# A written-out order for the first 1400 operations, early loads that wait for older ones, and masks and coefficients stored behind unit 0's values

## The chip, the cores and the metric

The kernel runs on one core of a Trainium2 chip. The core has a matrix engine (PE), a vector engine (DVE), an activation engine (ACT), a general engine (POOL) and a queue engine (SP) that issues transfers; each runs its own instructions strictly in the order in which they were written, and waits on semaphores for the others. 16 DMA engines move the data. The metric is device time in microseconds (us) per execution, lower is better.

## The reference

Attention over 8 batches, 8 heads, 576 positions and 64 features, with a local mask (32 keys back for half of the heads, 32 keys in steps of 4 for the others), and behind it a two-layer network whose activation is a rational function with learned coefficients:

```python
scores = np.where(masks, q @ k.T / 8, -1e9)
x = softmax(scores) @ v                 # (4608 tokens, 512)
h = x @ w_in                            # 512 -> 2048
P = a[0] + a[1]*h + a[2]*h**2 + a[3]*h**3
Q = 1 + abs(b[0])*abs(h) + abs(b[1])*h**2
out = (P / (Q + 1e-6)) @ w_out          # 2048 -> 512
```

`w_in` and `w_out` arrive in 64 bits and are turned into 32-bit numbers on the core.

## The kernel before, in words

**Units.** The attention is cut into 48 units, six for each of 8 batches (unit n = 6b + u). A unit loads its queries and keys (`qk`, 448 KB) and its values (`v`, 384 KB); then PE adds the mask and makes scores, DVE takes the maximum (`mx`), ACT the exponential, DVE the sum (`sm`) and its reciprocal, POOL or ACT divides (`p`), PE transposes (`t`, copied to `pT`), PE multiplies with `v`, and the result is split into a high and a low half, `xh` and `xl`. Units 0 to 5 (batch 0) write their halves straight from PSUM; the later ones go through DRAM (`results<-y`, then `z<-results`).

**Weights.** 16 blocks of `w_in` (`wi`) and 16 of `w_out` (`wo`), 512 KB each. Every block is loaded (`wi_raw`), scaled on ACT (`wi_f`), joined with its low bits (a multiply and shift on DVE), copied to a high half (ACT, DVE or POOL) and subtracted to a low half (DVE or POOL).

**Tiles.** 9 groups of 512 tokens times 16 blocks give 144 tiles. For each, PE makes `h` in 12 matmuls of 128x512; ACT and DVE work out the rational function (on DVE five passes at the least: `t<-t,h`, `h<-t,na_t,h`, `h<-h,na_t,r`, `a<-a,r`, `a<-a,h`; the product `a<-r,a` and the low half `gl` go to DVE or POOL); and PE adds the tile into four sums in 12 more matmuls (`out`). The first 8 tiles use batch 0, the next 16 batch 1, then the rest of batch 0, and so on. `h` and the transposes `t` share two PSUM banks in turn, so transpose 11, the last of the units of batch 1, waits until DVE is done with tile 1, and tile 2's `h` comes right behind it.

**What sets the order.** All work is a list of operations with an allowed set of engines, a cost and a due time (`Plan.op`). `Plan.run` steps through it before anything runs: it looks for the operation that can start first by its own costs, among those within 200 ns takes the one that is due first, and records its instructions. What is recorded on an engine stays in that order. Where PE would wait in the plan, before 150 us of it, `keep_busy` records matmuls on constants that nobody reads (128x512 bf16, of `ident_b`). All loads and stores are issued from SP through `load` and wait there for nothing but buffers and data.

Of the kernel before, what the change touches and what calls it, by code (L numbers as in the profile page):

```python
# [25 lines left out]
BOTH = {"ACT": 480, "DVE": 520}  # L26
# [5 lines left out]
DUE = [(-38.49, 8.95), (-134.53, 10.99), (409.06, 77.81), (48.99, 2.72), (456.65, -31.55), (557.24, -11.85), (83.16, -17.62), (714.91, 29.14)]  # L32

LATE = {"ab": -275.92, "ql": -296.25, "pl": 24.3, "qq": -47.45, "t1": 94.47, "t2": -169.93, "ln": 295.15, "ex": -497.79, "g0": -1.51, "g1": -59.76, "g2": -270.73, "gh": -314.62, "gl": 497.37, "out": 3.78}
SLACK = {"sc": 1.16, "qk0": -46.44, "v0": -50.35, "load": -3.46, "wi": 11.08, "wo": -0.87, "w": -17.68, "gl": -7.82, "out": -4.87}
# [4 lines left out]

DEPTH, LOADS, STAGE, AHEAD, ON_PE, BY_PE = 2, 2, 6, 6, 2, 2
LEFT = S - 512
RQ, RKEY, NV = 4 * 3 * 32, 4 * 128, 3 * 2 * 2 * 64
# [18 lines left out]

class Op:
# [4 lines left out]
    def __init__(self, engs, rank, fn, deps, dma, lock):  # L68
        self.engs, self.rank, self.fn, self.dma, self.lock = engs, rank, fn, dma, lock
        self.deps = [d for d in deps if d is not None]  # L70
        self.takes, self.follows = [], []
        self.spare = None
# [9 lines left out]
class Plan:  # L82
# [7 lines left out]
    DMA_START, DMA_NS, DMA_RATE = 1000.0, 1700.0, 380.0  # L90
# [5 lines left out]
    def op(self, engs, rank, fn, *deps, dma=0, lock=False):  # L96
        o = Op(engs, rank, fn, deps, dma, lock)
        self.ops.append(o)
        return o
# [32 lines left out]
    def run(self):  # L132
        free = {}
        pipe, ports = self.DMA_START, 0.0
# [6 lines left out]
        ready = [o for o in self.ops if not left[id(o)]]  # L141
        done = 0
        while ready:
            options = []
            for o in ready:
                before = list(o.deps)
                for tag, _ in o.takes:
                    bufs, groups = self.tags[tag]
                    if len(groups) >= bufs:
                        users = groups[len(groups) - bufs]  # L150
                        if any(u.end is None for u in users):
                            break
                        before += users
                else:
                    for eng, ns in o.engs.items():
                        shared = ports if Plan.shares(o, eng) else 0.0
                        t = max([free.get(eng, 0.0), shared] + [d.after(eng) for d in before])
                        options.append((t, o, eng, ns))
# [943 lines left out]
```

## Time and profile before

| | |
|---|---|
| runs | 913.08, 913.37, 917.36 us; median 913.37 us |
| profiled execution | span 911.9 us from first to last instruction; the median run is 1.5 us more than this span, which is taken as what lies around it |
| PE busy | 887.7 us (97%) |
| DVE, ACT, POOL busy | 727.6, 684.8, 472.8 us |
| moved | 103.46 MB, mean 113 GB/s |

A busy PE is no measure of work done here, since the matmuls on constants count too, and a matmul at half clock counts double. What matters is at which time a given tile starts, and which engine had no idle time before it.

### The profile page before, as it was taken

How to read it: one execution, taken by the hardware profiler on the slowest of the kernel's cores; microseconds unless marked ns; L12 is line 12 of the kernel's file. 1: busy time of each engine (PE TensorE's matmuls, PEld its weight loads, DVE VectorE, ACT ScalarE, POOL GpSimd, SP SyncE). 2: the span in 40 equal slices, each digit the busy share in tenths (PEclk: the TensorE clock that was granted, in tenths of full speed). 3: DMA queues.
4: the chain of work that ended last, by engine and by line, in shares of the span. 5: the costliest groups of instructions: out<-in, count | busy, mean ns of one | idle time of the engine just before them, and what ended most of it. 6: DMA issues, size and time to landing. Idle time of an engine off the chain costs nothing.

```text
span 911.9 us, 21320 instructions
## 1 busy us (share of the span) xinstructions
PE 887.7 (97%) x8208; PEld 714.9 (78%) x8208; DVE 727.6 (80%) x1291; ACT 684.8 (75%) x1128; POOL 472.8 (52%) x424
## 2 busy tenths in 40 slices
PE   6889999999999999999999999999999999999998
PEld 4656778877887888888888878888888888888876
DVE  4889999988998986888688886887688677566656
ACT  3888899867767777677767767777877788778774
POOL 2354666635555654555555555456455555544442
PEclk8899999999999999999999999999999999999999
DMA  9785614144643531453155441233143220001001
GB/s 339 272 281 181 241 55 147 60 127 143 192 141 113 152 93 46 131 165 112 49 173 156 135 141 65 96 104 98 47 145 108 63 70 1 0 1 47 1 1 46
DMA packets 85478, 103.46 MB, mean 113 GB/s; under 512 B 37377, under 2 KB 62849, under 8 KB 85377
## 3 DMA queue, kind: packets, MB, share of 16 engines
q1 hardware_dynamic: 85376, 102.11, 35.1%
q8 instruction: 64, 1.05, 0.5%
q14 instruction: 38, 0.30, 0.1%
HBM read 75.21 MB, written 26.87 MB: 112 GB/s over the span
## 4 chain that ended last, share of the span: by engine, by line
PE 82%; DVE 8%; DMA 4%; ACT 2%; issue 2%; POOL 1%; SPq 1%; DVEq 0%; ACTq 0%; POOLq 0%
PE out L245 39%; PE h L245 38%; PE pair L245 4%; DVE a L254 2%; DMA results<-y 1%; DVE h L254 1%; DMA z<-results 1%; ACT r L248 1%; DMA qk<-in_qk_dram 1%; DVE t L251 1%; SPq L242 1%; POOL a L257 1%; PE pair_A L245 0%; DVE a L251 0%; PE pair_B L245 0%
## 5 line engine op out<-in xcount | busy, mean ns | idle before, releaser
L245 PE MATMUL h<-xh,wi 128*128 128x512 f32 x1136 | 376.7, 393 | 5.5 <-DVE a L254 5.1
L245 PE MATMUL out<-gh,wo 128*128 128x512 f32 x1136 | 352.8, 392 | 0.0
L257 POOL TENSOR_TENSOR a<-r,a 128x512 f32<-128x512 f32 x123 | 159.2, 1294 | 259.4 <-ACT r L248 241.2
L245 PEld LDWEIGHTS h<-xh,wi 128*128 128x128 f32 x1136 | 213.3, 188 | 55.2 <-DVE a L254 9.3
L245 PEld LDWEIGHTS out<-gh,wo 128*128 128x128 f32 x1136 | 211.6, 188 | 44.9
L245 PE MATMUL out<-gl,wo 128*128 128x512 f32 x568 | 221.4, 390 | 0.6 <-POOL gl L257 0.6
L245 PE MATMUL h<-xl,wi 128*128 128x512 f32 x568 | 221.3, 390 | 0.0
L257 POOL TENSOR_TENSOR gl<-a,gh 128x512 fp32r<-128x512 f32 x137 | 182.0, 1329 | 40.9 <-ACT gh L248 31.0
L254 DVE SCALAR_TENSOR_TENSOR a<-a,r 128x512 f32<-128x512 f32 x141 | 101.4, 719 | 121.3 <-ACT r L248 119.3
L248 ACT ACTIVATE r<-a,ln_bias 128x512 f32<-128x512 f32 x141 | 101.8, 722 | 67.9 <-POOL a L257 64.5
L248 ACT ACTIVATE r<-a,ab_t 128x512 f32<-128x512 f32 x141 | 114.6, 813 | 14.6 <-DVE h L254 9.0
L245 PEld LDWEIGHTS out<-gl,wo 128*128 128x128 f32 x568 | 106.6, 188 | 23.7 <-POOL gl L257 1.2
L245 PEld LDWEIGHTS h<-xl,wi 128*128 128x128 f32 x568 | 106.7, 188 | 21.3
L248 ACT ACTIVATE a<-h 128x512 f32<-128x512 f32 x140 | 83.3, 595 | 52.4 <-PE h L245 44.2
L254 DVE SCALAR_TENSOR_TENSOR h<-t,na_t,h 128x512 f32<-128x512 f32 x142 | 107.3, 755 | 4.6
L248 ACT ACTIVATE t<-h,na_t 128x512 f32<-128x512 f32 x142 | 109.2, 769 | 1.6 <-DVE h L254 1.2
L254 DVE SCALAR_TENSOR_TENSOR h<-h,na_t,r 128x512 f32<-128x512 f32 x142 | 106.5, 750 | 4.6 <-ACT r L248 3.3
L248 ACT ACTIVATE r<-r,exp_bias 128x512 f32<-128x512 f32 x144 | 104.3, 724 | 4.7
L248 ACT ACTIVATE gh<-a 128x512 fp32r<-128x512 f32 x133 | 83.6, 628 | 27.0 <-PE out L245 24.5
L251 DVE TENSOR_TENSOR t<-t,h 128x512 f32<-128x512 f32 x142 | 95.9, 675 | 5.9 <-ACT t L248 4.9
L254 DVE SCALAR_TENSOR_TENSOR a<-a,h 128x512 f32<-128x512 f32 x140 | 96.2, 687 | 4.8
L257 POOL TENSOR_TENSOR xl<-z,xh 128x256 fp32r<-128x256 f32 (+5 forms) x52 | 39.1, 764 | 33.1 <-ACT xh L248 32.7
(123 smaller groups left out, 716.2 us busy)
## 6 DMA issues: line engine op xcount, KB each, us to landing
qk<-in_qk_dram SPq DMA_DIRECT2D x48, 448.0 KB, 5.3
v<-in_vp_dram SPq DMA_DIRECT2D x48, 384.0 KB, 3.9
out_dram<-os SPq DMA_DIRECT2D x36, 256.0 KB, 2.1
wi_raw<-in_w_in_dram SPq DMA_DIRECT2D x16, 512.0 KB, 6.2
wo_raw<-in_w_out_dram SPq DMA_DIRECT2D x16, 512.0 KB, 5.9
results<-y SPq DMA_DIRECT2D x42, 192.0 KB, 3.5
z<-results SPq DMA_DIRECT2D x168, 48.0 KB, 2.0
turned<-u SPq DMA_DIRECT2D x36, 192.0 KB, 2.2
```

The source lines that it names most:

```text
L242: pin(nc.sync.dma_start(dst, src))
L245: pin(nc.tensor.matmul(o, lhs, rhs, start=start, stop=stop, skip_group_check=free))
L248: pin(nc.scalar.activation(o, i, func, **kw))
L251: pin(nc.vector.tensor_tensor(o, x, y, op))
L254: pin(nc.vector.scalar_tensor_tensor(o, x, s, y, op0, op1))
L257: pin(nc.gpsimd.tensor_tensor(o, x, y, op))
```

## The change

Four things change together.

1. The first 1400 operations, up to about tile 45, are taken from a written list `ORDER`, where a letter can fix the engine (a ACT, d DVE, p POOL); the planner goes on from there with other due times and lateness constants (`DUE`, `LATE`, `SLACK`) and some other costs.
2. Each of the first 120 transfers waits in SP for an older one: the youngest of those behind which 1.2 MB or more have been issued since. With transfers of 384 to 512 KB that leaves three older ones unfinished while a fourth is issued. What follows on SP waits with it.
3. The masks and the six coefficients are no transfers of their own any more. They lie behind unit 0's values in one tensor (`head`, 128x966), which is now loaded first. POOL copies the masks out for the later units (`mask_t`, 128x384), and `make_coefs` stands later on DVE and ACT.
4. The planner, where it places work or counts matmuls on constants, knows the transfers in flight and PE's instruction pages (`fetched`).

```diff
-BOTH = {"ACT": 480, "DVE": 520}
+BOTH = {"ACT": 375, "DVE": 465}
...
+IN_FLIGHT, FLIGHTS = 1200000, 120
...
+ORDER = """
+3 2 19 18 0 6 33 32 7 8 9 10 49 1 4 11 12 20 21 48 13 22 23 34 24 25 35 14a 36 15 50 16 17 26 37 27 38 65 64 80 51 28a 39 79 96 52 53 66 40 67 54 29
...
+""".split()
...
+        for item in order:
+            n, eng = (int(item[:-1]), ENGINES[item[-1]]) if item[-1] in ENGINES else (int(item), None)
+            o = self.ops[n]
+            assert id(o) in ready, "the order breaks a dependency"
+            place(*next(x for x in options(o) if eng in (None, x[2])))
+        while ready:
...
+    flying = []
+
     def load(dst, src):
-        pin(nc.sync.dma_start(dst, src))
+
+        i = nc.sync.dma_start(dst, src)
+        pin(i)
+        ahead = 0
+        for before, size in reversed(flying if len(flying) < FLIGHTS else []):
+            if ahead >= IN_FLIGHT:
+                tc.add_manual_dep(i.ins, before.ins.name, mybir.DependencyInfo(mybir.DependencyClass.Sync, mybir.DependencyReason.SCHED_ONLY), reason="short queue")
+                break
+            ahead += size
+        flying.append((i, 4 * math.prod(dst.shape)))
...
         def load_v(self, pool, tag):
-            self.v = pool.tile([P, NV], F32, tag=tag, name=f"v{self.n}", bufs=LOADS if pool is att else 1)
-            load(self.v, vp[self.n])
+            if self.n:
+                self.v = pool.tile([P, NV], F32, tag=tag, name=f"v{self.n}", bufs=LOADS if pool is att else 1)
+                load(self.v, vp[self.n - 1])
+                return
+            t = pool.tile([P, NV + NMASK + 6], F32, tag=tag, name="v0", bufs=1)
+            load(t, head)
+            self.v = t[:, :NV]
+            extra["mask"] = t[:, NV : NV + NMASK].bitcast(BF16).rearrange("p (m k) -> p m k", k=64)
+            extra["coef"] = t[:, NV + NMASK :]
...
+            if self.n == 0:
+                copies.append(op({"POOL": 500}, -30, lambda e: copy(e, mask_t, extra["mask"]), lv))
+                copies.append(op({"DVE": 80}, -30, lambda e: make_coefs(), lv, consts))
...
-    masked = op({"SP": 430}, -39.4, lambda e: load(mask_t, mask), dma=P * 768)
-    lc = op({"SP": 60}, -39.5, lambda e: load(coef_t, coef), dma=3000)
...
-    plan.run()
+    plan.run(ORDER if wide else [])
```

**SP, the loads behind unit 4's keys.** Before, from the first weights on (`v5` are the values of unit 5, the last of batch 0):

```order
L242 DMA wi_raw0_181<-in_w_in_dram 128x512
L242 DMA wi_raw1_183<-in_w_in_dram 128x512
L242 DMA wi_raw2_187<-in_w_in_dram 128x512
L242 DMA wi_raw3_216<-in_w_in_dram 128x512
L242 DMA qk6_220<-in_qk_dram 128x896
L242 DMA qk7_223<-in_qk_dram 128x896
L242 DMA left_80<-l2_492 128x2x64
L242 DMA wi_raw4_548<-in_w_in_dram 128x512
L242 DMA left_80<-l3_576 128x2x16
L242 DMA qk8_614<-in_qk_dram 128x896
L242 DMA wi_raw5_620<-in_w_in_dram 128x512
L242 DMA v5_622<-in_vp_dram 128x768
```

After, the same place:

```order
L335 DMA v4_320<-in_vp_dram 128x768
L335 DMA qk4_322<-in_qk_dram 128x896
L335 DMA v5_324<-in_vp_dram 128x768
L335 DMA qk5_332<-in_qk_dram 128x896
L335 DMA wi_raw0_334<-in_w_in_dram 128x512
L335 DMA wi_raw1_410<-in_w_in_dram 128x512
L335 DMA qk6_412<-in_qk_dram 128x896
L335 DMA wo_raw0_450<-in_w_out_dram 128x512
```

The values of unit 5 have moved ahead of all weights, values stand ahead of the keys of the same unit, and the first block of `wo` has come up between the blocks of `wi`.

**PE, from the scores of unit 1 to the transposes of unit 0** (`pair`, `pair_A`, `pair_B` are PSUM banks for scores and results, `t0` is unit 0's transpose). Before:

```order
L245 MATMUL pair_85<-qk1_121 32x64 x24
L245 LDWEIGHTS ident_b_91
L245 MATMUL pair_A_99<-ident_b_91 128x512
L245 LDWEIGHTS ident_b_91
L245 MATMUL pair_A_99<-mask_t_89,ident_b_91 128x192
L245 MATMUL pair_A_99<-qk2_125 32x64 x24
L400 MATMUL t0_262<-ident_90,p0_218 128x128 x3
```

After:

```order
L346 MATMUL pair_85<-qk1_106 32x64 x24
L509 MATMUL t0_215<-ident_90,p0_164 128x128 x3
L346 LDWEIGHTS ident_b_91
L346 MATMUL pair_A_98<-v0_100,ident_b_91 128x192
L346 MATMUL pair_A_98<-qk2_160 32x64 x24
L346 MATMUL pair_B_99<-pT0_254,v0_100 64x32 x24
```

The transposes of unit 0 no longer stand behind the scores of unit 2, and its product with the values follows those scores, ahead of unit 3's. (Of the pairs of mask matmuls one is shown.) Over the whole program the matmuls on constants go from 55 to 30; from tile 2's `h` on from 19 to none.

**DVE, around the second weight block for `w_out`, between tiles 0 and 1.** Before:

```order
L251 TENSOR_TENSOR xl1_1062<-z7_1045,xh1_1061 128x2x192
L254 SCALAR_TENSOR_TENSOR wo_f1_1041<-wo_f1_1041,wo_raw1_708 128x512
L260 CAST wo1_1131<-wo_f1_1041 128x512
L251 TENSOR_TENSOR wo1_1131<-wo_f1_1041,wo1_1131 128x512
L254 SCALAR_TENSOR_TENSOR wo_f2_1072<-wo_f2_1072,wo_raw2_714 128x512
L452 STREAM_TRANSPOSE y9_1199<-pair_85 128x2x96 x2
```

After, between the same two tiles:

```order
L355 SCALAR_TENSOR_TENSOR wo_f4_861<-wo_f4_861,wo_raw4_800 128x512
L355 SCALAR_TENSOR_TENSOR wo_f2_943<-wo_f2_943,wo_raw2_710 128x512
L355 SCALAR_TENSOR_TENSOR wo_f3_965<-wo_f3_965,wo_raw3_742 128x512
L454 TENSOR_REDUCE mx10_1069<-pair_85 128x6
L561 STREAM_TRANSPOSE y8_1073<-pair_85 128x2x96 x2
L352 TENSOR_TENSOR wo4_1067<-wo_f4_861,wo4_1067 128x512
L352 TENSOR_TENSOR wo2_1084<-wo_f2_943,wo2_1084 128x512
L352 TENSOR_TENSOR gl0_1088<-a0_842,gh0_1052 128x512
```

The casts have left DVE for POOL, the low half `gl0` of tile 0 has come over from POOL, and the blocks are taken in another order.

## Rows read from the trace of the kernel before

**Rows 1.** The page: the span; busy time of PE; PE in 40 equal slices (9 is 90% or more); the instruction queue of the transfers (packets, MB, share of 16 engines); the chain of work that ended last, by engine.

```profile
span 911.9 us, 21320 instructions
...
PE   6889999999999999999999999999999999999998
...
q8 instruction: 64, 1.05, 0.5%
...
PE 82%; DVE 8%; DMA 4%; ACT 2%; issue 2%; POOL 1%; SPq 1%; DVEq 0%; ACTq 0%; POOLq 0%
```

**Rows 2.** The engines' busy time in stretches of the first 200 us. Columns: stretch, its length, busy us and (instructions) of PE, of PE's weight loads, DVE, ACT, POOL; then the granted clock (1.00 is 2.4 GHz, 0.50 is 1.2 GHz), the share of the DMA engines, GB/s.

```profile
0.00:7.00 7.00, 5.54 (x65) 2.49 (x66) 0.28 (x2) 1.49 (x2) 1.87 (x13) 1.00 0.69 203
7.00:20.00 13.00, 7.78 (x286) 5.77 (x285) 8.70 (x23) 4.21 (x9) 3.28 (x4) 0.87 1.03 404
20.00:40.00 20.00, 16.04 (x471) 12.06 (x471) 14.75 (x34) 15.37 (x52) 5.82 (x9) 0.83 0.71 251
40.00:60.00 20.00, 16.82 (x292) 11.46 (x272) 17.02 (x35) 17.70 (x47) 12.43 (x13) 1.00 0.88 308
60.00:70.00 10.00, 8.90 (x222) 6.24 (x222) 8.74 (x19) 8.46 (x18) 3.33 (x3) 1.00 0.77 259
70.00:140.00 70.00, 65.92 (x377) 51.10 (x377) 67.99 (x109) 61.84 (x104) 41.37 (x34) 1.00 0.45 159
140.00:200.00 60.00, 60.00 (x536) 49.06 (x535) 56.13 (x94) 48.75 (x77) 32.40 (x25) 1.00 0.34 109
```

**Rows 3.** PE's instructions in order of time: start, length, what, and in brackets the idle time just before and what ended it ("issue" is time in which PE waited for nothing that the profile shows).

```profile
8.99 0.72 PE L245 MATMUL pair<-qk 64*32 64x64 f32 x48 [1.64 <-DMA qk<-in_qk_dram]
...
11.98 0.90 PE L400 MATMUL t<-ident,p 128*128 128x128 f32 x3
...
17.11 0.66 PE L245 MATMUL pair_B<-pT,v 64*64 64x32 f32 x30
21.16 0.61 PE L245 MATMUL pair_B<-pT,v 64*64 64x32 f32 x18 [3.39 <-issue]
...
42.23 0.53 PE L245 MATMUL h<-xh,wi 128*128 128x512 f32 x1
...
57.20 0.50 PE L245 MATMUL h<-xh,wi 128*128 128x512 f32 x1 [1.17 <-DVE a L254]
...
69.75 0.47 PE L245 MATMUL h<-xh,wi 128*128 128x512 f32 x1
...
78.02 1.47 PE L245 MATMUL out<-ident_b,zeros_b 128*128 128x512 bf16 x6
```

**Rows 4.** DVE's instructions in order of time: behind PE's long wait, the maximum of unit 5, the last passes of tiles 1 and 10, and between them a product on DVE.

```profile
22.33 0.56 DVE L251 TENSOR_TENSOR xl<-pair_B,xh 128x384 fp32r<-128x384 f32 x1 [3.30 <-ACT xh L248]
23.86 0.56 DVE L345 TENSOR_REDUCE mx<-pair 128x6 f32<-128x384 f32 x1 [0.97 <-PE pair L245]
...
68.57 0.69 DVE L254 SCALAR_TENSOR_TENSOR a<-a,h 128x512 f32<-128x512 f32 x1
...
75.76 0.69 DVE L251 TENSOR_TENSOR a<-r,a 128x512 f32<-128x512 f32 x1
...
131.02 0.69 DVE L254 SCALAR_TENSOR_TENSOR a<-a,h 128x512 f32<-128x512 f32 x1
```

**Rows 5.** SP's issues in order of time: the last of the first run of loads (keys of units 6 and 7), the values of units 5, 6 and 7, and those of unit 10.

```profile
14.85 1.41 SPq L242 DMA_DIRECT2D qk<-in_qk_dram  x2
...
30.95 3.25 SPq L242 DMA_DIRECT2D v<-in_vp_dram  x3
...
60.93 1.27 SPq L242 DMA_DIRECT2D v<-in_vp_dram  x1
```

**Rows 6.** DMA queues in two stretches: 14 to 18 us, where only the data queue q1 moved anything, and the instruction queue q8 from 18 to 21.2 us: packets, MB, share of 16 engines.

```profile
q1 hardware_dynamic: 490, 1.66, 102.9%
...
q8 instruction: 1, 0.02, 2.1%
```

**Rows 7.** Transfers issued in the first 20 us: count, KB each, median us from issue to landing.

```profile
qk<-in_qk_dram SPq DMA_DIRECT2D x8, 448.0 KB, 8.7
...
v<-in_vp_dram SPq DMA_DIRECT2D x5, 384.0 KB, 8.0
```

**Rows 8.** The same for 45 to 80 us, with what the queues moved there in all.

```profile
DMA packets 5579, 10.05 MB, mean 287 GB/s; under 512 B 1699, under 2 KB 3363, under 8 KB 5574
...
v<-in_vp_dram SPq DMA_DIRECT2D x4, 384.0 KB, 4.6
wi_raw<-in_w_in_dram SPq DMA_DIRECT2D x3, 512.0 KB, 6.0
```

**Rows 9.** DVE's groups by shape, 20 to 140 us: count, busy us, mean ns of one, idle us before them.

```profile
L254 DVE SCALAR_TENSOR_TENSOR wi_f<-wi_f,wi_raw 128x512 int32<-128x512 int32 x16 | 13.8, 864 | 0.1
...
L251 DVE TENSOR_TENSOR a<-r,a 128x512 f32<-128x512 f32 x10 | 8.7, 868 | 0.6 <-ACT r L248 0.4
...
L260 DVE CAST wo<-wo_f 128x512 fp32r<-128x512 f32 x4 | 1.7, 427 | 0.1
...
L251 DVE TENSOR_TENSOR xl<-z,xh 128x256 fp32r<-128x256 f32 x2 | 1.1, 527 | 0.9 <-ACT xh L248 0.9
```

**Rows 10.** Busy time in the stretch from 180 to 280 us, columns as in rows 2.

```profile
180.00:280.00 100.00, 99.29 (x1065) 80.01 (x1065) 90.59 (x171) 69.64 (x113) 50.95 (x48) 1.00 0.50 149
```

More of the change, by code (lines that the diff above doesn't have):

```diff
@@ L140, in run @@
                 after.setdefault(id(d), []).append(o)
[L141 to L158, printed above, removed]
-            assert options, "the plan is stuck"
-            first = min(x[0] for x in options)
-            eng0 = min((x for x in options if x[0] == first), key=lambda x: x[1].rank)[2]
-            start, o, eng, ns = min(
-                (x for x in options if x[2] == eng0 and x[0] <= first + self.WINDOW), key=lambda x: (x[1].rank, x[0])
-            )
@@ new lines, in run, with options @@
+        ready = {id(o): o for o in self.ops if not left[id(o)]}
+        def options(o):
+            before = list(o.deps)
+            for tag, _ in o.takes:
+                bufs, groups = self.tags[tag]
+                if len(groups) >= bufs:
+                    users = groups[len(groups) - bufs]
+                    if any(u.end is None for u in users):
+                        return
+                    before += users
+            queue = []
+            if o.dma:
+                ahead, parts = 0, 0
+                for f in reversed(flying):
+                    if (ahead >= IN_FLIGHT and len(flying) < FLIGHTS) or parts + f.parts + o.parts > self.FLYING:
+                        queue = [f.end]
+                        break
+                    ahead, parts = ahead + f.dma, parts + f.parts
+            for eng, ns in o.engs.items():
+                shared = state["ports"] if Plan.shares(o, eng) else 0.0
+                yield max([free.get(eng, 0.0), shared] + queue + [d.after(eng) for d in before]), o, eng, ns
@@ L165, in run, with place @@
+        def place(start, o, eng, ns):
             for tag, users in o.takes:
@@ L183, in run @@
                 if not left[id(n)]:
-                    ready.append(n)
-        assert done == len(self.ops), "the plan is stuck"
+                    ready[id(n)] = n
+        for item in order:
[4 more added lines that the diff above has]
+        while ready:
+            every = [x for o in ready.values() for x in options(o)]
+            assert every, "the plan is stuck"
+            first = min(x[0] for x in every)
+            eng0 = min((x for x in every if x[0] == first), key=lambda x: x[1].rank)[2]
+            place(*min((x for x in every if x[2] == eng0 and x[0] <= first + self.WINDOW), key=lambda x: (x[1].rank, x[0])))
+        assert not state["left"], "the plan is stuck"
 @with_exitstack
@@ L667, in finish @@
                 plan.takes(self.placed[0], *(("p", 2) if self.n % 2 else ("pT", 1)), [av])
[L668 removed]
+            plan.takes(self.lv, self.vt, 1 if start else LOADS, [av] if self.n else [av, *copies[:2], *mask_users])
             if b not in x_done:
```

199 lines of the change are left out of this document (136 added, 63 removed).

## The prediction

> **What bounds the kernel now.** The page first [rows 1]. PE is busy for 887.7 of 911.9 us, the chain that ended last lies on PE for 82%, and in the 40 slices only the first three or four are not full. From there on nothing but PE's own work sets the time, and both orders hold the same real matmuls. So the change can act only at the start, and the question is when PE gets into its full stride.
>
> Next the stretches [rows 2]. PE idles 5.2 us of 7 to 20 us, 4.0 and 3.2 us of the next two twenties, 4.1 us of 70 to 140, and nothing from 140 to 200. Who is full there instead? DVE: 14.75 of 20 us, then 17.02 of 20, 8.74 of 10, and from 70 to 140 us 67.99 of 70. ACT is next with 61.84, POOL far behind. So I read the run-up as DVE's: first DVE waits for data and for PE, then it is full until PE has caught up near 140 us.
>
> Then PE in order of time [rows 3]. The first tile starts at 42.23 us, the second at 57.20, the third (tile 2) at 69.75 us. Tile 2's `h` stands right behind transpose 11, which waits for DVE's last pass of tile 1; that pass starts at 68.57 and ends at 69.26 us [rows 4]. I use these two places as marks: tile 1's last pass on DVE, and tile 2's start on PE, 0.5 us later. From tile 2's start to the end it is 911.9 - 69.75 = 842.2 us.
>
> What delays DVE up to 69.26 us? Its idle time by stretch is 6.7 (0 to 7), 4.3 (7 to 20), 5.25 (20 to 40), 3.0 (40 to 60) and 1.3 us (60 to 70): 20.5 us, of which 6.7 is the wait for the first scores. The largest piece has one cause: PE stands still for 3.39 us in the middle of unit 2's product with no wait that the profile names ("issue"), then DVE idles 3.30 us for the result [rows 3, 4]. In this time the data queue takes the 16 engines fully (102.9%), and PE's wait ends behind the arrival of one packet of 16 KB on the instruction queue, in 18 to 21.2 us; there was none in the four us before [rows 6]. So PE ran out of instructions. The half clock of the following stretches (0.83 on average from 20 to 40 us [rows 2]) comes behind this stop.
>
> **Step a, the shorter queue.** By the end of the first run of issues, 16.3 us [rows 5], SP had asked for 8 `qk`, 5 `v`, 4 blocks of weights and the mask: 7.8 MB. Moved by then were 7 x 0.203 + 9.3 x 0.404 = 5.2 MB [rows 2], so 2.7 MB stood in line, 6.6 us at 404 GB/s; loads took 8.0 to 8.7 us to land [rows 7]. After the change at most three older loads and the one just issued are open, 1.3 to 1.7 MB, 3.2 to 4.2 us. If the instruction packet waits in proportion to the line, it comes 2.4 to 3.4 us earlier and the stop of 3.39 us shrinks to between 0 and 1.0. Bounds: 0 (it does not wait for the data) and -3.4. I take **-2.9 us**, nearer the full effect, because the packet came just when the line was longest.
>
> The Trainium skill speaks against this step. "DMA: Bandwidth & Descriptors", section "Queues, rings and completion order", says that each DMA engine takes turns between queue rows packet by packet; by that an instruction packet would wait for one data packet and never for a line, step a would be 0, and the total below would be 2.9 us later. The row of 3.39 us doesn't fit a wait of one packet, but no row shows when the packet was asked for.
>
> **Step b, DVE's other idle time before tile 1.** 13.8 - 3.3 = 10.5 us. Two moves bear on it. Unit 0's transposes leave their place behind unit 2's scores: they ran at 11.98 us although unit 0's division on POOL was through earlier, and unit 2's scores only started when its keys landed. And `v5`, which stood behind six weight blocks and was issued at 30.95 us [rows 5], now stands ahead of all weights, so that unit 5 (its maximum at 23.86 us [rows 4]) need not wait until 37 us for its product. Bounds: 0 and -10.5. Filling the pipeline with the first two units, and the round trip of the results through DRAM, stay; I take **-3.0 us**, under a third.
>
> **Step c, DVE's work before that mark.** Counted in both orders up to tile 1's last pass: three casts fewer (0.43 each [rows 9], 1.3), one copy of `pT` fewer (0.5, as a pass of 384 elements [rows 4]), two `xl` products fewer (0.53 [rows 9], 1.1) against two short `xl` copies and three small ones more (0.8), one join more (0.7, like any pass of 512 that is not disturbed [rows 4]), and two products `a<-r,a` and one `gl` more (2.1). Three halves of `wi` give way to three of `wo`. Sum: **+0.7 us**.
>
> **Step d, DVE from tile 1 to tile 10.** Between the two last passes of [rows 4] lie 62.5 us, with DVE full. Of its work there the new order takes away five casts (2.1), four joins (2.8), two halves of `wo` (1.4) and three `xl` products (1.6), 7.9 us; it adds one `a<-r,a`, three `gl` and three halves of `wi`, 4.8 us: **-3.1 us**. Bounds: 0, if something else fills the gap, and -8.6, since PE has 4.1 us of idle time from 70 us on [rows 2] and 19 matmuls on constants, 1.47 us per six [rows 3], which the new order does not hold. Joins and `a<-r,a` average 0.86 us [rows 9] where an undisturbed pass takes 0.69 [rows 4], so they meet other work; I count no gain on that.
>
> **At nothing.** The mask's copy on POOL hides in POOL's idle time (3.28 busy of 13 us); without that cover it costs some 0.7 us before unit 0's division. `make_coefs` moves to where only tile 0 needs it. Unit 0's scores now need `v` and `qk`, 0.9 MB; PE is busy with constants until 5.9 us either way. Behind tile 45 PE was full and stays so.
>
> **Step e, what is given back.** Up to tile 36 the new order has put eight `a<-r,a` and seven `gl` more on DVE, and, since units 12 to 17 stand later, some of their passes fall there too: by the same durations about 8 us more than before between tiles 20 and 36, where DVE has 9.4 us idle in 100 [rows 10]. That just fits; I take 0.
>
> **Sum.** -2.9 - 3.0 + 0.7 - 3.1 = -8.3 us. 911.9 - 8.3 = 903.6 us of span; the median run is 1.5 us above the span, so about **905 us**, ratio 0.991. A change of under 0.5% (4.6 us) is what a measurement of this kernel can hardly tell from none.
>
> **The rivals.**
> *More than that.* If the new order leaves DVE only the 6.7 us at the start and two or three for filling, b becomes -7, and d goes to PE's limit, -6: 911.9 - 2.9 - 7 + 0.7 - 6 = 896.7, a run of 898 us. For it: in the new order no matmul on constants stands behind tile 2, so its planner saw no gap there. Against it: the order is fixed from costs, and each deviation makes an engine wait.
> *The instructions come no sooner.* Step a is 0 and half of b goes with it, since the stop moves into other units: 911.9 - 1.5 + 0.7 - 3.1 = 908.0, a run of 909.5 us.
> *DVE becomes the bound of tiles 20 to 36.* If DVE there is busy 97% at most, as from 70 to 140 us, (90.6 + 8) / 0.97 is 101.7 us for 100, and with joins and locks as slow as in [rows 9] up to 4 us: a run of 907 to 909 us.
> *The short queue starves the loads (the other side).* Up to unit 10's values SP's new order asks for 13 `qk`, 11 `v`, 17 weight blocks and some results, 20.2 MB; behind them come the landing, unit 10's product, unit 12's scores and transpose 11, some 1.7 us, then tile 2. At 404 GB/s that is no limit (1.2 + 50 + 1.7 = 53 us). With three loads of 0.44 MB open and landings of 4.6 us [rows 8] it is 287 GB/s, the same as the mean of 45 to 80 us: 1.2 + 70.4 + 1.7 = 73.3 us, 3.5 later than now, and with step d no change. It is slower by 4.6 us if tile 2 starts later than 77.4 us, under 271 GB/s; at 250 GB/s tile 2 starts at 83.7 us and the run takes 913.4 + 14.0 - 3.1 = 924 us. For it: three loads at the 6.0 us of `wi` [rows 8] would be 230 GB/s. Against it: landings of 6 us were themselves a line, and with a fourth issued while three are open, 1.7 MB over 4.6 us is 380 GB/s.
>
> **Chances.** The forecast (901 to 908.8 us) 0.45, more 0.19, instructions no sooner 0.14, DVE later 0.10 (a third of it still under 908.8), loads starved 0.12. Faster by over 0.5%: 0.45 + 0.19 + 0.03 = 0.67; slower: 0.12, and 0.01 for the rest; within: 0.20. The range of eight in ten goes from 894, near the bounds of b and d together, to 918, where only the starved loads are left out.
>
> **What would show it.** Right: no stop of over 1 us without a named releaser on PE before 25 us; loads of the first 20 us landing in 4 to 5 us instead of 8 to 9; tile 0 near 35 to 38 us and tile 2 near 64 us; no matmul on constants behind it; PE full from about 130 us. Wrong: the stop still there; DMA under 300 GB/s in the first 20 us, with PE or DVE waiting for `qk`, `v` or weights; DVE at 98% from 180 to 280 us with PE idle for it.

## The result: 918.9 us, 0.6% slower

The changed kernel takes 918.93 us (median of 7 runs, 918.2 to 922.32) against 913.37 us: ratio 1.0062, interval 1.0041 to 1.0083. The forecast was 905 us, the range 894 to 918. The profiled execution has a span of 916.6 us (918.4 us in all), 4.7 us more than before [rows 1].

The page after: the span, PE in 40 slices, the instruction queue, the chain by engine, PE's first products with what they waited for.

```profile
span 916.6 us, 21251 instructions
...
PE   7879999989999999999999999999999999999998
...
q8 instruction: 64, 1.05, 0.5%
...
PE 63%; DVE 18%; ACT 6%; DMA 5%; issue 4%; SPq 2%; POOL 1%; ACTq 0%; DVEq 0%; POOLq 0%
...
L346 PE MATMUL h<-xh,wi 128*128 128x512 f32 x1136 | 378.5, 394 | 8.9 <-DVE a L355 8.5
```

DVE's share of the chain has gone from 8 to 18%, and there is a slice that is not full behind the start. The stretches, columns as in [rows 2, 10]:

```profile
0.00:7.00 7.00, 5.54 (x61) 2.39 (x64) 0.00 (x0) 1.28 (x1) 2.39 (x14) 1.00 0.74 255
7.00:20.00 13.00, 8.85 (x326) 6.70 (x321) 8.62 (x23) 3.83 (x8) 3.31 (x4) 0.95 0.98 358
20.00:40.00 20.00, 17.20 (x478) 13.70 (x477) 16.06 (x40) 15.95 (x54) 9.57 (x12) 0.86 0.88 324
...
60.00:70.00 10.00, 6.50 (x117) 5.27 (x118) 8.05 (x16) 7.23 (x18) 2.48 (x3) 0.83 0.54 157
70.00:140.00 70.00, 68.44 (x385) 54.53 (x385) 67.11 (x101) 60.24 (x99) 39.93 (x38) 1.00 0.44 148
140.00:200.00 60.00, 56.07 (x421) 44.11 (x421) 58.89 (x89) 45.34 (x71) 27.26 (x23) 1.00 0.23 68
180.00:280.00 100.00, 94.89 (x1132) 75.39 (x1131) 93.73 (x182) 67.58 (x109) 52.75 (x49) 1.00 0.55 164
```

From 7 to 40 us and from 70 to 140 PE is busier than before; from 40 to 60 us it is not (16.53 us busy against 16.82). The loss stands in 60 to 70 us (6.50 of 10) and from 140 us on: 56.07 of 60 where it was 60.00, with DVE at 58.89 and POOL at 27 of 60. PE in order of time, answering [rows 3]; the fourth line is tile 1, the last tile 2:

```profile
18.76 0.86 PE L346 MATMUL pair_B<-pT,v 64*64 64x32 f32 x21 [1.72 <-issue]
25.22 1.23 PE L346 MATMUL pair_A<-pT,v 64*64 64x32 f32 x46 [1.51 <-issue]
...
37.79 0.50 PE L346 MATMUL h<-xh,wi 128*128 128x512 f32 x1
...
52.39 0.48 PE L346 MATMUL h<-xh,wi 128*128 128x512 f32 x1
...
66.38 0.78 PE L346 MATMUL pair<-v,pT 64*32 64x64 f32 x44 [3.16 <-ACT xh L349]
...
68.36 0.78 PE L346 MATMUL h<-xh,wi 128*128 128x512 f32 x1
```

Tiles 0 and 1 come 4.4 and 4.8 us earlier, tile 2 only 1.4: a stop of 3.16 us is in between. And the marks on DVE, the last passes of tiles 1 and 10 (68.57 and 131.02 us in [rows 4]):

```profile
64.06 0.69 DVE L355 SCALAR_TENSOR_TENSOR a<-a,h 128x512 f32<-128x512 f32 x1
...
124.22 0.69 DVE L355 SCALAR_TENSOR_TENSOR a<-a,h 128x512 f32<-128x512 f32 x1
```

4.5 us earlier at the one mark and 6.8 at the other. In this profile the gain that was forecast for tile 10 (8.3 us) nearly came, and it was lost behind it. But this profile is the earliest of nine that have the same instructions up to tile 12 on PE, DVE, ACT and POOL (last section): the others reach tile 12 up to 4.2 us later, so the early part of the lead is to be read as 3 to 7 us and not as 7.

**A ledger by tile.** The trace holds all products `h<-xl`, four for each tile that uses the `h` banks, so the product numbered 4n is tile n's. Start of that product, in us; "cut at 12" is an experiment below whose program is the same up to tile 12:

| tile | before | after | after less before | list cut at 12 |
|---|---|---|---|---|
| 0 | 42.59 | 38.12 | -4.5 | 38.27 |
| 2 | 70.06 | 68.93 | -1.1 | 69.04 |
| 12 | 132.68 | 125.35 | -7.3 | 125.44 |
| 31 | 245.82 | 246.56 | +0.7 | 241.61 |
| 141 | 894.74 | 899.22 | +4.5 | 892.20 |

Between tiles 12 and 31 the change loses 8.1 us, behind that 3.7. The first of these losses is steady: from tile 12 to 31 it is 121.2 us after and 120.3 to 121.7 in three runs below that have the same instructions there (`v10` first, the missing waits, the old late numbers), against 113.1 us before and 112.0 in the old order with waits. The engines' busy time up to tile 12 and from there to tile 31, before:

```profile
0.00:132.70 132.70, 113.70 (x1658) 83.06 (x1659) 110.45 (x205) 101.83 (x216) 62.82 (x71) 0.96 0.66 234
132.70:245.80 113.10, 112.39 (x1033) 91.05 (x1032) 104.07 (x186) 90.04 (x147) 63.99 (x55) 1.00 0.43 130
```

and after:

```profile
0.00:125.30 125.30, 108.48 (x1632) 81.89 (x1633) 104.55 (x197) 94.07 (x202) 60.49 (x75) 0.96 0.72 253
125.30:246.60 121.30, 114.70 (x1034) 90.88 (x1034) 116.63 (x200) 88.69 (x142) 60.45 (x54) 1.00 0.34 101
```

Read DVE's column. At tile 12 DVE has done 104.55 us of work instead of 110.45, and stood idle 20.75 us instead of 22.25. Of the 7.4 us of lead, 5.9 is work that DVE has not done and 1.5 is idle time saved. Part of that work has left DVE for good: it casts no block of weights up to tile 12, where it cast eight before (3.4 us); in the whole program it casts two and not nine. Five low halves `xl<-z` (3.4 us) have gone to POOL, and four `gl` (3.2 us) have come from there. Part is only put off: 12 joins of `wi` are done and not 15. In the next stretch DVE is busy 12.6 us longer and idle 4.4 us less: 8.2 us. What the work is, the groups of that stretch tell; before:

```profile
L254 DVE SCALAR_TENSOR_TENSOR a<-a,r 128x512 f32<-128x512 f32 x19 | 13.0, 685 | 0.0
...
L251 DVE TENSOR_TENSOR a<-r,a 128x512 f32<-128x512 f32 x9 | 6.2, 693 | 2.3 <-ACT r L248 1.3 <-POOL wo L257 0.5
L251 DVE TENSOR_TENSOR gl<-a,gh 128x512 fp32r<-128x512 f32 x3 | 2.1, 713 | 0.0
...
L254 DVE SCALAR_TENSOR_TENSOR wi_f<-wi_f,wi_raw 128x512 int32<-128x512 int32 x1 | 0.7, 650 | 0.0
```

and after:

```profile
L355 DVE SCALAR_TENSOR_TENSOR a<-a,r 128x512 f32<-128x512 f32 x19 | 15.9, 834 | 0.2 <-ACT r L349 0.2
L352 DVE TENSOR_TENSOR a<-r,a 128x512 f32<-128x512 f32 x13 | 10.9, 839 | 0.3 <-ACT r L349 0.3
...
L355 DVE SCALAR_TENSOR_TENSOR wi_f<-wi_f,wi_raw 128x512 int32<-128x512 int32 x5 | 4.5, 906 | 0.0
L352 DVE TENSOR_TENSOR gl<-a,gh 128x512 fp32r<-128x512 f32 x5 | 4.4, 886 | 0.0
L352 DVE TENSOR_TENSOR wi<-wi_f,wi 128x512 fp32r<-128x512 f32 x2 | 2.4, 1176 | 0.0
```

Three sources (lengths of neighbours overlap a little, so the groups add up to more than the busy time): weights put off, 3.8 + 2.4 (the two halves `wi` are also such as POOL did before: ten in the whole program, eight after); passes that POOL did before, 4.7 for `a<-r,a` and 2.3 for `gl`; and the same 19 passes `a<-a,r`, 2.9 us longer.

### The profile page after: what moved, and what is told of

It reads as the page before. It is cut to its first block, busy times and chain, and to the rows that moved or that the text cites. A ratio compares the mean times of both kernels' runs of the same rounds, so it can differ in the third digit from the quotient of the medians.

```text
span 916.6 us, 21251 instructions
## 1 busy us (share of the span) xinstructions
PE 886.5 (97%) x8183; PEld 712.3 (78%) x8183; DVE 739.4 (81%) x1314; ACT 677.8 (74%) x1115; POOL 458.8 (50%) x415
## 4 chain that ended last, share of the span: by engine, by line
PE 63%; DVE 18%; ACT 6%; DMA 5%; issue 4%; SPq 2%; POOL 1%; ACTq 0%; DVEq 0%; POOLq 0%
PE h L346 30%; PE out L346 29%; DVE a L355 5%; DVE h L355 4%; PE pair L346 4%; ACT r L349 3%; SPq L335 2%; DMA z<-results 2%; DVE t L352 2%; DMA qk<-in_qk_dram 2%; DVE a L352 1%; DMA results<-y 1%; DVE wo_f L355 1%; ACT p L349 1%; POOL a L358 1%
## 5 line engine op out<-in xcount | busy, mean ns | idle before, releaser
L358 POOL TENSOR_TENSOR a<-r,a 128x512 f32<-128x512 f32 x115 | 148.9, 1295 | 271.1 <-ACT r L349 267.5
L358 POOL TENSOR_TENSOR gl<-a,gh 128x512 fp32r<-128x512 f32 x130 | 173.7, 1336 | 52.4 <-ACT gh L349 36.9
L349 ACT ACTIVATE r<-a,ab_t 128x512 f32<-128x512 f32 x141 | 114.8, 814 | 27.1 <-DVE a L355 13.9
L349 ACT ACTIVATE t<-h,na_t 128x512 f32<-128x512 f32 x142 | 109.7, 773 | 17.1 <-PE h L346 11.8
L355 DVE SCALAR_TENSOR_TENSOR a<-a,r 128x512 f32<-128x512 f32 x141 | 103.6, 735 | 0.7 <-ACT r L349 0.7
L358 POOL TENSOR_TENSOR p<-p,sm 128x384 f32<-128x384 f32 x42 | 35.8, 855 | 32.0 <-DVE sm L494 17.9
```

The source lines that it names most:

```text
L349: pin(nc.scalar.activation(o, i, func, **kw))
L355: pin(nc.vector.scalar_tensor_tensor(o, x, s, y, op0, op1))
L358: pin(nc.gpsimd.tensor_tensor(o, x, y, op))
```

## The experiments

All ratios are to the kernel before, timed beside each kernel; the changed kernel's is 1.0062.

### The transfers: values ahead of results

PE's stop at 63 to 66 us is for `v10`. SP issues it behind four transfers for `z7`, and these stood until POOL's last pass over a `wo` tile gave a staging buffer back. POOL, then SP:

```profile
58.22 1.59 POOL L358 TENSOR_TENSOR wo<-wo_f,wo 128x512 fp32r<-128x512 f32 x1
```

```profile
59.84 2.58 SPq L335 DMA_DIRECT2D z<-results  x4
62.46 0.43 SPq L335 DMA_DIRECT2D v<-in_vp_dram  x1
```

In the run with ten passes moved to POOL (below), whose program is the same up to here, the profile puts the same stop (3.44 us) down to `v`. The first experiment moves one entry of the list:

```
- ... 331 176p 343 378 ...      (331: z7, 343: v10)
+ ... 343 331 176p 378 ...
```

> The changed kernel, with one entry of its list moved: the load of v10 stands ahead of the four z7 transfers on SP, not behind them. Theory A (SP stands for z7 until GpSimd's last pass over a wo tile gives a buffer back, and v10 behind it comes late for unit 10's product): v10 is issued near 57.5 us and not at 62.5, lands near 62, the TensorE stop of 3.2 us before unit 10's product shrinks below 1 us, tile 2 starts 2 to 3.5 us earlier (65 to 66 us), and as far as VectorE does not take it back the time falls by 1 to 3 us against the changed kernel (to about 916 to 918). Rival B (VectorE is the bound from there on, so that an earlier tile 2 only waits later): tile 2 comes earlier but the time stays within 1 us of the changed kernel's 918.9. Rival C (z7 itself or the buffer is what unit 10 waits for): the stop stays at 3 us.

Measured: 1.0076 (1.0058 to 1.0094), no gain. `v10` was issued at 59.18 us, the stop was gone, and tile 2 came 12.6 us behind tile 1, not 16.2. Then PE stopped for the next unit's values instead:

```profile
79.05 0.91 PE L346 MATMUL pair<-v,pT 64*32 64x64 f32 x45 [3.05 <-DMA v<-in_vp_dram]
```

From tile 1 to tile 5 it took 33.3 us, with `v10` in its old place 31.7 (30.7 to 32.9 in the nine profiles). Theory A holds for the stop and fails for the time; of the expectations rival B's is nearest, for another reason: the next load in the same row is late.

### The waits of the transfers, added and taken away

First the kernel before with nothing but the waits in `load`:

```
+        for before, size in reversed(flying if len(flying) < 120 else []):
+            if ahead >= 1200000:
+                tc.add_manual_dep(i.ins, before.ins.name, ..., reason="short queue")
```

> The kernel before, its own order on every engine, with only the waits of the changed kernel's loads added (a load among the first 120 waits until no more than about 1.2 MB stand ahead of it). If a shorter queue by itself brings units' values and instruction blocks sooner: landings in the first 20 us fall from 8 to 5 or 6 us, the 3.39 us fetch stop shrinks or splits, tile 0 starts 1 to 4 us earlier than 42.2, and the time is 0 to 3 us shorter than the kernel before. Rival (the waits starve the transfer engines early, and the list is what the earlier tile 0 comes from): tile 0 no earlier or later, the time the same or up to 4 us longer.

Measured: 1.0011 (0.9995 to 1.0026). PE's stop without a named releaser and the landings of the first 20 us:

```profile
18.84 0.53 PE L257 MATMUL pair_B<-pT,v 64*64 64x32 f32 x18 [1.76 <-issue]
```

```profile
qk<-in_qk_dram SPq DMA_DIRECT2D x8, 448.0 KB, 5.3
```

Loads land in 5.3 us, not 8.7 [rows 7], and the stop is 1.76 us, not 3.39 [rows 3]. But PE waits 3.0 us for keys where it waited 2.5, and tile 0 starts 0.5 us later. The shorter queue does to the landings what was thought, and is worth nothing in this order. That it also shortens the stop is not shown: that is one profile of each, and the run whose list is cut at tile 16, with the same waits and keys landing in 5.0 us, has the stop at nearly its old length:

```profile
21.67 0.86 PE L346 MATMUL pair_B<-pT,v 64*64 64x32 f32 x21 [3.42 <-issue]
```

Then the changed kernel without them, all instructions in the same order:

```
-            if ahead >= IN_FLIGHT:
+            if ahead >= 10**9:
```

> The changed kernel without the waits that keep the early transfers' queue short; all five engines' instructions stand in the same order as in the changed kernel. If the waits shorten the queue and so the landings (qk 5.5, v 5.2 us in the first 20 us): landings go back to 8 to 10 us, the fetch stops of TensorE come together again near 20 us (3 us or more), tile 0 starts within 1.5 us of the changed kernel's 37.8 us, and the time is 0 to 2 us longer. Rival (the waits starve the transfer engines: 255 GB/s in the first 7 us against 404): without them the units' values come sooner in the first 20 us, tile 0 starts 1 to 3 us earlier, and the time is 1 to 3 us shorter, 916 to 918.

Measured: 1.0107 (1.0088 to 1.0125), slower than the changed kernel by 0.45%. Keys land in 8.8 us, tile 0 starts at 41.74 and tile 12 at 130.8 us (125.3 to 129.5 in the nine profiles with waits). The first theory has the direction. It missed the size (some 4 us, not 0 to 2), and the stops that were to come together into 3 us or more were 1.41 and 2.03 us. So the list is better with its waits, though in the old order they bring nothing; by what they help is not shown.

### Ten passes back to POOL

```
- 1204d 1239d 1311d 1356d 1374d 1383d 1401d 1482d 1491d 1500d
+ 1204p 1239p 1311p 1356p 1374p 1383p 1401p 1482p 1491p 1500p
```

> The changed kernel, with ten passes of tiles 7 to 22 given from VectorE to GpSimd as they stood in the kernel before: five gl (tiles 8, 12, 16, 17, 22) and five products a<-r,a (tiles 7, 15, 16, 22, 23). VectorE loses about 5 x 0.70 + 5 x 0.74 = 7.2 us of work up to 220 us. Theory A (VectorE is the bound of the changed kernel from 100 to 240 us): TensorE's waits on VectorE between 140 and 240 us (6.5 us) fall to 2 us or less and the time falls by 4 to 7 us, to 912 to 915. Rival B (what bounds there is not VectorE's work but the order in which its passes stand, or the later transfers): the time stays within 1.5 us of 918.9. Rival C (GpSimd's passes take 1.3 us in place of 0.7 and hold the port that VectorE's passes need): no gain or a loss, VectorE's busy share unchanged because its own passes get longer.

Measured: 1.0045 (1.0027 to 1.0063), which cannot be told from 1.0062. From tile 12 to tile 31:

```profile
127.90:246.90 119.00, 114.85 (x1034) 90.66 (x1033) 111.59 (x192) 88.42 (x142) 71.15 (x62) 1.00 0.35 103
```

DVE is busy 5.0 us less than after, POOL 10.7 us more, and the stretch is 2.3 us shorter, not 5. One reason can be read in the trace of after, DVE first, then POOL:

```profile
191.59 1.74 DVE L352 TENSOR_TENSOR a<-r,a 128x512 f32<-128x512 f32 x1
193.25 1.78 DVE L355 SCALAR_TENSOR_TENSOR wo_f<-wo_f,wo_raw 128x512 int32<-128x512 int32 x1
```

```profile
191.49 1.30 POOL L358 TENSOR_TENSOR gl<-a,gh 128x512 fp32r<-128x512 f32 x1
192.74 1.74 POOL L358 TENSOR_TENSOR wo<-wo_f,wo 128x512 fp32r<-128x512 f32 x1
```

A product that takes 0.69 us alone [rows 4] takes 1.74 when POOL's pass began 0.1 us ahead of it, and the two engines go on in turns. The Trainium skill has this as a rule ("SBUF — State Buffer", section "SBUF: two separate sides": the port pair that DVE and GpSimd share is an exclusive lock, and of a GpSimd pass that reads SBUF and a DVE pass with two inputs there, whichever starts first holds it for the whole instruction); the trace agrees: DVE's product ends at 193.33 us, 0.54 us behind the end of POOL's pass (192.79). So a pass moved to POOL is not simply gone from DVE: with these ten moved, the joins of `wo` took 1170 ns on average, not 1063.

Both edits together (the ten letters and `v10` first):

> The two edits together: v10 ahead of z7, and the ten passes on GpSimd. If both causes are as theory A has them, the gains add: about 3 us at tile 2 and 4 to 7 us between 140 and 240 us, so 908 to 912, faster than the kernel before by 0.2 to 0.6%. If VectorE's work is the only bound, this run is as fast as the one with the passes alone (within 1 us). If neither is a cause, 918 to 920.

Measured: 1.0070 (1.0044 to 1.0097). No sum of gains, since neither edit had one.

### DVE's work taken away, nothing moved

```
+        def product(self, eng):
+            n = slice(0, 64 if eng == "DVE" and 12 <= self.i < 32 else 512)
+            either(eng, self.a[:, n], self.r[:, n], self.a[:, n], ALU.mult)
```

> The changed kernel, every instruction in its place and on its engine, but thirteen products a<-r,a that VectorE does in tiles 12 to 23 and 30 work on 64 of their 512 columns, so that a part of the computation is left out. VectorE loses about 13 x (0.82 - 0.15) = 8.7 us of work between tile 12 and tile 31 and nothing else is changed. Theory V (VectorE's work bounds that stretch): tile 31 comes 6 to 9 us earlier after tile 12 (112 to 115 us after it, not 121.2), and the time falls by 5 to 9 us, to 910 to 914. Theory P (what bounds is the places: passes wait for other engines' results in a fixed row): VectorE's idle time grows by most of it, tile 31 comes less than 4 us earlier, and the time falls by under 4 us.

```profile
126.60:242.50 115.90, 112.59 (x1034) 91.22 (x1033) 109.76 (x200) 88.56 (x142) 60.44 (x54) 1.00 0.35 106
```

```profile
L352 DVE TENSOR_TENSOR a<-r,a 128x64 f32<-128x64 f32 x12 | 5.1, 422 | 1.1 <-ACT r L349 1.0
```

The short products still took 422 ns, so only 5.1 us of products went (10.9 to 5.8 with the one left whole), not 8.7. DVE's busy time fell by 6.9 us and the stretch by 5.4. With every place and engine unchanged, 5.4 us of 6.9 came back: DVE's work bounds tiles 12 to 31, nearly as theory V has it (112 to 115 us; 115.9 measured). In the time less remained: 1.0022 (1.0008 to 1.0036), some 3 to 4 us better than after, which is in the range of theory P.

### The list cut at tile 12, and at other tiles

```
-    plan.run(ORDER if wide else [])
+    plan.run(ORDER[:557] if wide else [])
```

> The changed kernel with its list cut at tile 12: the planner with the new numbers sets the order and the engines from there. Theory L: about 6 us of VectorE work is owed at tile 12 whoever orders it, so tile 31 comes at 244 to 248 us, and the time differs from the changed kernel by what the planner's choice of engines saves VectorE between tiles 12 and 31 (up to 8 us of passes): 912 to 919. Rival O (the list's order is what loses it): tile 31 near 239 and the time 908 to 911.

Measured: 1.0001 (0.9988 to 1.0014). The program is that of the change up to tile 12, and in the profile it reaches tile 12 at the same time (125.4). Then:

```profile
125.40:241.60 116.20, 113.97 (x1129) 92.08 (x1129) 109.41 (x194) 91.86 (x149) 77.50 (x69) 1.00 0.44 136
```

5.1 us shorter than after, with 7.2 us less on DVE and 17.1 more on POOL. Rival O is right that the list's own choice from tile 12 on loses 5 us; theory L is right that even a better one pays some of the lead back, since before needs 113.1 us: the lead is 7.2 us at tile 12, 4.2 at tile 31 and 2.5 at tile 141. (The profiled execution, 911.3 us, was among the quickest of this kernel, whose median is 914.3.)

The other cuts have 290, 446, 654 and 752 entries:

> The changed kernel with its list cut at tile 2 (290 entries). If the list's own order from tile 2 on is no better than the planner's, this run is as fast as the one cut at tile 12 (914.3, within 1.5 us) or faster; if the lead at tile 12 (5 us of equal work) is the list's doing and can be kept, it is 2 to 5 us slower than that one.

> The list cut at tile 8 (446 entries). By the same reasoning: within 1.5 us of the run cut at tile 12 if neither the list nor the planner gains between tiles 8 and 12; 916 to 919 if the list's entries of tiles 8 to 12 carry the gain; 910 to 913 if these entries already put VectorE's work off.

> The list cut at tile 16 (654 entries). Cut at tile 12 the time is 914.3, cut at tile 20 it is 922.8, whole 918.9. If the loss is made by entries between tiles 12 and 16: 917 to 923; if it is made later: 913 to 916.

> The changed kernel with its list cut at tile 20 (752 entries), not at tile 12; the planner with the new numbers sets the rest. Against the kernel before, the changed one leads by 5.9 us at tile 20 and by nothing at tile 31; with the list cut at tile 12 the lead at tile 31 is 4.2 us. If the loss is made by the order that the list sets between tiles 20 and 31: this run is as fast as the one cut at 12, 913 to 916. If what the list owes at tile 20 (VectorE's work there is 160.7 us against 164.8, two units fewer by tile 23) must be paid whatever comes after: tile 31 at 245 to 247 and 917 to 919.

| cut at tile | ratio | tile 12 | 12 to 31 | DVE busy in it | 31 to 141 |
|---|---|---|---|---|---|
| 2 | 1.0036 (1.0020 to 1.0052) | 131.0 | 114.8 | 108.47 | 649.2 |
| 8 | 1.0046 (1.0030 to 1.0063) | 131.1 | 119.7 | 111.10 | 648.1 |
| 12 | 1.0001 (0.9988 to 1.0014) | 125.4 | 116.2 | 109.41 | 650.6 |
| 16 | 1.0098 (1.0078 to 1.0119) | 128.1 | 117.8 | 107.86 | 661.8 |
| 20 | 1.0092 (1.0072 to 1.0113) | 127.0 | 117.1 | 112.59 | 657.1 |
| whole list | 1.0062 (1.0041 to 1.0083) | 125.3 | 121.3 | 116.63 | 652.7 |

(The cuts at 2, 8 and 12 have 96 matmuls of units less to do behind tile 31, some 1.4 us.) The cuts at 2 and 8 came out where the expectations put a list whose entries up to tile 12 carry the gain (918.2 and 918.7 us), and they reach tile 12 later than any of the nine. The cuts at 16 and 20 (923.7 and 922.8 us) lie outside all that was expected: up to tile 31 they stand no worse than the whole list, and behind it, in the planner's part, they lose 9.1 and 4.4 us more. So no place in the list is shown to be where the loss begins. What the table does show: lists with the same first 557 entries differ by 9 us (1%), more than the whole gain that they make early.

### Engines without the order

The changed kernel's order for all 3750 operations, with the engines of the run cut at 12 for 42 of them:

```
- 1311d 1383d 1401d 1491d ...
+ 1311p 1383p 1401p 1491p ...   (42 such letters behind entry 557)
```

> The changed kernel's whole order, kept entry for entry on all of its 3750 operations, with other engines alone: between tile 12 and the end of the list 42 operations run where the planner put them in the run whose list was cut at tile 12 (VectorE gives GpSimd six gl, four products a<-r,a and three weight passes, and gets three gl and one product back; ScalarE and GpSimd change eleven gh). Theory E (the engines: too many passes on VectorE between tiles 12 and 31): the lead of 7.3 us at tile 12 is kept to 4 us or more at tile 31 and the time is near that of the cut list, 913 to 916. Theory P (the places: the list's order itself, in which passes of attention and weights stand ahead of the pass that TensorE waits for): VectorE's work at tile 31 falls from 238 to about 230 us but its idle time grows by as much, tile 31 stays at 245 to 248, and the time at 917 to 920.

Measured: 1.0150 (1.0126 to 1.0174). DVE busy 5.4 us less than after, the stretch 4 us longer:

```profile
128.50:253.80 125.30, 114.91 (x1034) 90.53 (x1033) 111.27 (x187) 89.57 (x144) 74.38 (x66) 1.00 0.33 98
```

The same engines in the planner's own order gave 116.2 us. Theory P is right that fewer passes on DVE do not help by themselves; the loss is larger than it expected (917 to 920 us). The list's places and these 42 letters do not go together. It is not so of every letter: six of the 42 are among the ten above, which cost nothing. (In this run, the next one and the three parts, matmuls on constants are allowed up to 112 us of the plan and not 150; none stands behind tile 2 in any of them, nor in after.)

### The old order behind a new beginning

The list to tile 12, and the order and engines of before behind it:

```
+ ORDER[:557], then what is left of the order of before
```

> The changed kernel's list as far as tile 12 (557 entries), and from there the remaining operations listed in the order and on the engines of the kernel before (what that one had already done by tile 12 comes first); transfers with their waits as in the changed kernel. At tile 12 the changed kernel stands 7.3 us ahead of the kernel before, but VectorE has done 111.8 us of work there and not 118.1 (three joins of wi fewer, the casts of wi and wo left for later). Theory L (the lead is a loan: VectorE is full on both sides, and what it has not done by tile 12 is done after it): the lead melts by about the 6.3 us owed within the next ten tiles, tile 31 stands within 2 us of the kernel before's 245.8, and the time is 912 to 915. Rival O (the lead is real and the list's own order after tile 12 wastes it): tile 31 stands 5 to 7 us ahead of the kernel before and the time is 906 to 908.

Measured: 1.0084 (1.0066 to 1.0101); neither theory. The work that the list had put off came ahead of the tiles in one piece, and PE stood for it:

```profile
139.06 0.80 PE L422 MATMUL out<-gl,wo 128*128 128x512 f32 x1 [6.40 <-POOL gl L434]
```

DVE is busy 109.4 us from tile 12 to 31, 5.3 more than in the same order before, with three joins of `wi` more: so work is owed at tile 12, but the price of 127.7 us for the stretch is that of the worst place to pay it.

Behind tile 31 the change loses 3.7 us more, with PE waiting for DVE's passes from 260 to 900 us, after and before:

```profile
PE h L346 <- DVE a L355: 2.1, 4, 1.0
PE pair L346 <- DVE pair L355: 0.5, 1, 0.5
```

```profile
PE pair L245 <- DVE pair L254: 0.7, 1, 0.7
```

Two runs were to tell whether the planner's new numbers do that. The whole list with the old late numbers behind it:

```
-LATE = {"ab": -3.96, ...}, DUE[2:] = [(29.12, -14.02), ...]
+LATE = {"ab": -275.92, ...}, DUE[2:] = [(409.06, 77.81), ...]
```

> The changed kernel with its whole list, and behind it (from tile 43 on) the planner with the kernel before's late numbers: all of LATE, and DUE of batches 2 to 7. The changed kernel loses 3.7 us against the kernel before between the last output of tile 31 (63.8 against 63.1 past 200) and the end, with the same number of units done at both. Theory N (the new numbers make the planner's order behind the list worse): the stretch from tile 47 to the end gets 1.5 to 2.5 us shorter and the time 1.5 to 2.5 us shorter than the changed kernel's 918.9. Rival (that loss comes from what the list leaves behind it, or from the profile chosen): no change, within 1 us.

Measured: 1.0175 (1.0159 to 1.0192), slower still; the old numbers behind the list cost some 10 us more. And the list to 12, the planner's order to tile 31, the order of before from there:

```
+ ORDER[:557], the planner's order of the cut run to tile 31, then the order of before
```

> Three parts: the list to tile 12, the planner's order with the new numbers from there to the last output of tile 31 (as in the run cut at tile 12), and from there the order of the kernel before to the end. In the run cut at tile 12 the lead over the kernel before is 5.8 us of equal work at 200 us and 3.5 at the end. Theory N (the planner's new numbers cost 2 to 3 us behind tile 31, through waits of TensorE on VectorE's passes): the lead at 250 us is kept to the end and the time is 909 to 912. Rival (what is lost there is owed, whatever order): 913 to 916.

Measured: 1.0003 (0.9987 to 1.0019): no better than the cut at 12 alone. With `v10` ahead of `z7` in it:

> The three parts, with the load of v10 ahead of the z7 transfers. In the run of that edit alone the 3.1 us stop of TensorE before unit 10's product was gone but one of 3.05 us stood before a later unit, and the time did not fall. If TensorE's early stops cost time only as far as VectorE is not the bound: within 1 us of the three parts alone. If the lead is kept by the planner's order: 1 to 3 us faster than the three parts alone, 907 to 910.

Measured: 0.9994 (0.9980 to 1.0009). The 3.7 us behind tile 31 are not owed from before it: the run with the old order behind tile 12 does the same 5460 matmuls on PE from tile 31 to 141 in 648.6 us, before took 648.9 and after 652.7. So they go with the order and the engines there. PE's waits account for some 1.9 of them; what in that order makes them stays open. No version was faster than the kernel before.

## Why the prediction was wrong

**The marks came in this profile, the first of them by luck.** a + b + c forecast -5.2 us at tile 1's last pass, -4.5 was measured; a to d -8.3 at tile 10's, -6.8 measured. In the nine profiles of the same instructions it is -4.5 to +0.1 at the first mark, in the middle -0.9, and -6.8 to -2.6 at the second, in the middle -4.8 (all against one profile of before). Only step d holds in all of them: from the one mark to the other DVE's work fell from 60.96 to 56.95 us (-4.0; d counted -3.1), and the time by 1.0 to 4.2 us, in the middle 3.2. Step c had the wrong sign: DVE did 47.21 us of work up to the first mark and not 48.78, where +0.7 was counted.

**Step e failed, at 0.** It stood for what is given back behind tile 20, and 8.1 us were given back between tiles 12 and 31. Under it lies the premise that the change can act only at the start: PE, full from 140 to 200 us before, was not so any more (56.07 of 60 us). Three things were left out of step e.
- The joins that step d took away from DVE before tile 10 do not vanish; they are the program's and come later (five of `wi` behind tile 12 and not one), and two halves of `wi` with them. d booked joins as gain, and e charged only the switched passes and the units' passes. (The casts, which d booked too, did leave DVE.)
- The idle time of 9.4 us [rows 10] was to take up 8 us of work. But a lead is itself time taken from DVE: to do 8 us more and stand 8 us earlier takes 16 us of idle time. DVE's ledger to tile 31 is the sum that should have been made: 6.7 us more work (221.2 against 214.5), 5.9 us less idle time, 0.8 us later. It holds 13 products and low halves that POOL did before (some 11 us); casts and `xl` that left DVE are the other side.
- Passes were priced at 0.7 us. On a DVE that is hardly idle (4.7 us of 121.3) beside a POOL that runs, they took 0.83 to 0.89 us.

**Steps a and b failed as well.** -5.9 us of idle time on DVE was forecast to go before tile 10. 1.5 us went by tile 12 in after; in the nine profiles DVE is idle for 20.8 to 24.2 us up to there, in the middle 22.4, where it was 22.25 before: on the whole nothing went. Step a alone (-2.9) is 0 within the interval: 1.0011. The stop was 3.39 us before, 1.76 with the waits, two stops of 1.72 and 1.51 us after, 3.42 us in the cut at 16 and, without waits, two of 1.41 and 2.03: no run shows that the line of loads sets its length, nor that it is for instructions. By the rule of the Trainium skill ("DMA: Bandwidth & Descriptors", section "Queues, rings and completion order") that a DMA engine takes turns between queues packet by packet step a would be 0, and the time agrees.

**Missed altogether:** the stop of 3.16 us for `v10` behind `z7` (1.5 to 3.5 us in the nine profiles). That PE stays full behind tile 45 was wrong: the change is 0.5 us late at tile 45 and 4.5 at tile 141.

**The rivals.** "DVE becomes the bound of tiles 20 to 36" was the right one, with a chance of 0.10 and a price of 907 to 909: it began at tile 12 and cost 8 us and not up to 4, so the time lies far above its price too. "The short queue starves the loads" did not happen: 358 GB/s from 7 to 20 us, landings of 5.5 us, and without the waits the kernel is slower.

**Its own signs.** No constants behind tile 2: came. Tile 0 at 37.79 us (35 to 38): came, by luck, since seven of the nine profiles have it at 39 to 41 us. Landings of 5.2 to 5.5 us for keys and values and 6.6 to 6.7 for weights (4 to 5): missed, in the right direction. No stop without a named releaser over 1 us, tile 2 near 64 us (68.4), PE full from 130 us: did not come. The sign against it, DVE at 98% with PE idle for it, was there, at 140 to 200 us (58.89 of 60) and not at 180 to 280.

## What to carry to other kernels

A lead on the engine that waits is worth only what the engine that it waits for has gained too: compare two orders at a tile by the busy time of the bound engine up to it, not by the clock. If that engine is full, work put off is a loan, and passes given to it must be paid at the price that they have when nothing is idle. Letters and places in a written-out order are one choice: the letters of one order at the places of another cost 8 us here, moving one load only moved the stop, and continuations of one beginning differed by more than the change was to bring. And before a lead of a few us is credited to a step, the same beginning has to be profiled more than once.

## What was not expected of the hardware

The same instructions up to tile 12 reached it between 125.3 and 129.5 us, in the middle at 127.4, in nine profiles (after, the cuts at 12, 16 and 20, the short products, the old late numbers, the 42 letters, the old order behind 12, the three parts); before reached it at 132.7. After is the earliest. Much of the difference is there at tile 0: 38.12 us in after and 40.59 in the three parts, 2.5 of the 3.9 us by which these two differ at tile 12. In 20 to 40 us the granted clock was 0.86 in after and 0.52 in the three parts:

```profile
20.00:40.00 20.00, 19.40 (x459) 16.30 (x461) 12.98 (x34) 14.74 (x50) 8.78 (x11) 0.52 0.87 318
```

0.52 is nearly the lower level (1.2 GHz) throughout, behind a stop of PE of 2.19 us at 17 to 19 us that the profile gives no releaser for; in after the stop there was 1.72 us. The clock is not all of it: the run with the old late numbers had 0.84 in this stretch and reached tile 12 at 127.4 us. So single profiles of this start differ by up to 4 us, and the step of -2.9 us that was forecast for it is within that.
